# Two heads of the second batch go through the opening path, and the order of the work is set with new numbers

## The chip, the cores and the metric

One core of a Trainium2 chip runs the whole kernel. The metric is the device time of one execution in microseconds (us); lower is better. The core has a matrix engine (PE, with PEld for its weight loads), three engines for elementwise work (DVE, ACT, POOL) and SP, which here only issues DMAs.

## What is computed

Eight batches, eight heads, 576 positions, head width 64, all in float32. Attention is causal by blocks of 64 positions; its output is the input of a gated MLP that mixes positions.

```python
scores = scale * np.matmul(q, k.transpose(0, 1, 3, 2))
scores = np.where(block_i >= block_j, scores, -1000000000.0)
scores = scores - np.max(scores, axis=-1, keepdims=True)
attn = np.exp(scores)
attn = attn / (np.sum(attn, axis=-1, keepdims=True) + 1e-09)
x = np.matmul(attn, v)                   # heads side by side: 576 x 512 a batch

h = np.maximum(x @ w_in, 0.0)            # 512 -> 1024
u, v = h[..., :512], h[..., 512:]
v_n = (v - mean(v)) / np.sqrt(var(v) + 1e-06)
v_s = np.einsum('ts,bsd->btd', w_spatial, v_n) + b_spatial[None, :, None]
out = (u * v_s) @ w_out
```

## The kernel before

**Units of work.** Heads are taken in pairs, four pairs a batch. A batch is four pairs of attention and one MLP (`moe`, L1072). The MLP is made of groups of PE matmuls: five `v_group` (tile `mv`), eight `u_group` (`mu`), eight `sp_group` (`ms`, mixing of positions) and eight `out_groups` (`mo`). Most factors are split into a high and a low part, and three products stand for one of full precision.

**Two ways through attention.** Batch 0 goes through `opening` (L807): ordinary 128x128 tiles; a pair is four units (`unit(k, pr)`), each with scores (L896, L906, tile `s`), row maxima (DVE, L934, L940), exponentials (ACT), sums and scaling (POOL or ACT), transposes of the probabilities on PE (L992, tile `t`), copies of these from PSUM to `pt` (L373) and the product with the values (L1020, tile `av`). Batches 1 to 7 go through `attention` (L526). There the keys of the two heads are interleaved in blocks of 16, the masked blocks are left out, and the transpose is done in two steps: DVE turns blocks of 32x32 (L713, seven instructions a pair) and SP issues 16 DMAs of 100 KB (L723) that move the blocks from `p` to `pt`. Then follow 22 matmuls `av` (L751). Batch 1 takes q and k as they are (`plain`); later batches split them.

**Buffers.** `pt` is one tile and so is `v`; `p` has two. The 16 DMAs of a pair can start when the pair before has read `pt` for its last product. The values `v` of a pair are loaded when the pair before has read its own. Results of attention go to six tiles `x` (tag `x` of `xt_p`), which the MLP reads.

**What sets the order.** Nothing is placed by hand. Each step is an `Op` with its engine, a duration in ns, what it waits for, the buffers that it takes and gives back, and a `rank`. `Line.play` (L215) walks through time with these numbers: of the steps that could start first on an engine, the one of lowest rank goes. PE has four lanes (`S` scores, `T` transposes, `A` products with the values, `M` MLP groups in the order of a string such as `"vuvuvuvuvuuuu"`); `SLACK` says by how much a lane must be ready ahead, `op.gate` ties scores and products to how much MLP work was done (`LEAD`, `MATE_LEAD`). Where the plan sees PE wait for over some 0.9 us, `bridge` (L173) puts matmuls on an identity there (`pad`, L353, L357) whose result nobody reads. The plan only gives the order; on the chip each engine takes its queue in that order and waits on semaphores.

```python
SLACK = {"A": 2500, "S": 1200, "T": 0, "M": 100}
n = int((until - now - 300) / PAD_NS)     # L173: number of pads
```

Of the kernel before, what the change touches and what calls it, by code (L numbers as in the profile page):

```python
# [38 lines left out]
LEAD = 6.0  # L39
MATE, MATE_LEAD = 8, 6.0  # L40

# [5 lines left out]
SLACK = {"A": 2500, "S": 1200, "T": 0, "M": 100}  # L47
# [54 lines left out]
class Line:  # L102
# [112 lines left out]
    def play(self):  # L215
        while True:
# [44 lines left out]
def kernel(  # L261
# [44 lines left out]
    mask0 = ff_p.tile([P, 512], F32, tag="vl3", name="mask0")  # L306
    nc.vector.memset(mask0, 0.0)
    nc.vector.memset(mask0[0:64, 448:512], -8.0e9)
# [59 lines left out]
    mask_hold = given(r_vn, 9 * NPAIR + 14)  # L368
# [39 lines left out]
    def prep_w(hi, lo, w, rows, cols, name, rank):  # L408
# [10 lines left out]
        f_hold = mask_hold if home else Hold(r_vr, 2)  # L419
# [106 lines left out]
    def attention(b, pr):  # L526
        g = b * NPAIR + pr
        plain = b == 1
        nm = f"{b}_{pr}"
        box = {}  # L530
# [15 lines left out]
        got = add("SP", 420, load_raw, takes=[raw_hold], rank=3, size=P * 4 * Q8)  # L546
        f_hold = Hold(r_f, 1)
        got_f = add("SP", 420, load_first, takes=[f_hold], rank=3, size=P * 4 * 2 * P)
        v_hold = Hold(r_v, 1)

        def load_v():
            box["v"] = v_p.tile([P, 9, P], F32, tag="v", name=f"v_{nm}")
            nc.sync.dma_start(box["v"], v[b, pr])

        got_v = add("SP", 420, load_v, takes=[v_hold], rank=1.5, size=P * 9 * P * 4)
# [4 lines left out]
        else:  # L560
# [93 lines left out]
        for k in range(3):  # L654
            for c, (m, hd) in enumerate(SETS[k]):
                w = 32 * m + 16 if m else 32

                def rows(k=k, c=c, m=m, hd=hd, w=w):
                    if "pp" not in box:
                        box["pp"] = p_p.tile([P, 4, NT, 32], F32, tag="p", name=f"p_{nm}")  # L660
                    if ("max", k) not in box:
# [9 lines left out]
                        drops=[s_hold[k][hd % 2]], rank=1)  # L671
# [11 lines left out]
                runs_of[k].append(add("ACT", 282 + 0.845 * 4 * w, exps, after=[a], rank=2))  # L683
        for k in range(3):
# [12 lines left out]
            a = add("POOL", 200, guard, after=runs_of[k], rank=2)  # L697
            a = add("DVE", 165, turn, after=[a], rank=1.5)
            for c, (m, hd) in enumerate(SETS[k]):
# [6 lines left out]
                muls[m, hd] = add(eng, ns, scale, after=[a], rank=3)  # L706
# [3 lines left out]
        for t0, t1, of in MOVES:  # L710
# [4 lines left out]
            done.append(add("DVE", 70 + 1.05 * P * (t1 - t0), blocks, after=[muls[x] for x in of], rank=3))  # L715
        for s in range(4):
            for i in (0, 2, 1, 3):
# [9 lines left out]
                moved.append(add("SP", 635, regroup, after=done, drops=[pp_hold], rank=2, size=102400,  # L727
# [49 lines left out]
        for z, (q0, n, src) in enumerate(((0, 320, al), (320, 256, ah))):  # L777
# [16 lines left out]
            h = add("ACT", (321, 269)[z], high, after=[src], takes=takes, drops=[a_holds[z]], rank=0,  # L794
                    behind=ev[:1])
            ev.append(add("DVE", (402, 335)[z], low, after=[h], drops=[a_holds[z]], rank=0))
# [8 lines left out]
        xs_done[b, pr] = add("POOL", 271, tail, after=ev, rank=2)  # L805

    def opening():  # L807

        boxes = [{} for _ in range(NPAIR)]
# [3 lines left out]
        pp_holds = [Hold(r_pp, 7), Hold(r_pp, 9)]  # L813

        def place(k, pr):

            if k < 2:
                return k, 3 * pr, 3
# [19 lines left out]
        def load_part(pr, n):  # L838
            spans = (slice(0, 256), slice(Q0, Q0 + 256)), (slice(256, Q0), slice(Q0 + 256, KQ))
            for m, cs in enumerate(spans[n]):  # L840
                def fn(cs=cs, start=n == m == 0):
                    if start:
                        boxes[pr]["raw"] = raw_tile(pr)
                    nc.sync.dma_start(boxes[pr]["raw"][:, cs], qk[0, pr, :, cs])
# [3 lines left out]
                    "SP", 340, fn, takes=takes,  # L848
                    rank=-4 + 0.01 * len(got), size=P * 4 * (cs.stop - cs.start)))

        def load_v(pr):
            def fn():
                if pr == 1:
                    t = boxes[pr]["v"]
                elif pr == 0:
# [18 lines left out]
        load_v(3)  # L874

        def unit(k, pr):
            nm = f"0_{pr}_{k}"
            box = dict(raw=boxes[pr])
            heads = ((0, SLOTS[2 * k][1], SLOTS[2 * k][2]), (1, SLOTS[2 * k][1], SLOTS[2 * k][2]))
# [47 lines left out]
            for r, (hd, o, n, at) in enumerate(runs):  # L927
                def rows(hd=hd, o=o, n=n, at=at, r=r):
# [10 lines left out]
                    else:  # L939
                        nc.vector.tensor_tensor_reduce(  # L940
                            out=out, in0=box["s"][hd][:, o:o + n], in1=mask0[:, 512 - n:512],
# [12 lines left out]
                a = add("DVE", 76 + 1.045 * n, rows, after=[op], drops=[s_hold[hd], mask_hold], rank=-2)  # L954
                sums.append(add("ACT", 282 + 0.845 * n, exps, after=[a], rank=-1))
            n = len(runs)

            def guard():
# [5 lines left out]
            a = add("POOL", 190, guard, after=sums, rank=-1)  # L964
            a = add("DVE", 165, lambda: nc.vector.reciprocal(box["sum"][:, 4:4 + n], box["sum"][:, 0:n]),
                    after=[a], rank=-1.5)
# [465 lines left out]
```

## Time and profile before

| | us |
|---|---|
| three runs | 674.37, 675.48, 675.71 (median 675.48) |
| the profiled execution | 673.02 |
| its span, first to last instruction | 671.0 |
| PE busy in the span | 652.9 |
| DVE, ACT, POOL busy | 484.7, 374.3, 321.9 |

The profiled execution has 2.02 us outside its span, and it is 2.46 us under the median of the three runs. "Busy" counts pads too, and the end of a matmul is modelled, so two neighbouring matmuls overlap in the records: the distance from the start of one to the start of the next is what one costs in a row of equal ones. A matmul in plain float32 has two records. "Idle" in front of an instruction names what ended it.

### The profile page before, as it was taken

What the parts mean: (1) busy time and instruction counts of PE and PEld (TensorE: products, weight loads), DVE (VectorE), ACT (ScalarE), POOL (GpSimd) and SP (SyncE); (2) the same over time, 40 slices, a digit from 0 to 9 for tenths busy, and PEclk for the clock granted to TensorE, in tenths of its full rate; (3) what the DMA queues carried; (4) which work ended last, traced back from release to release, by engine and by line L of the source; (5) the groups of instructions that cost most, each with busy time, mean ns of one, the idle gap of its engine ahead of it and who ended that gap; (6) DMA issues with size and microseconds to landing.
All of it is one profiled execution on the core that took longest, in us unless ns stands there. A gap on an engine that the chain in (4) does not pass through costs nothing.

```text
span 671.0 us, 16079 instructions
## 1 busy us (share of the span) xinstructions
PE 652.9 (97%) x5670; PEld 590.1 (88%) x5670; DVE 484.7 (72%) x1353; ACT 374.3 (56%) x1067; POOL 321.9 (48%) x631
## 2 busy tenths in 40 slices
PE   7999989889999999999999999999999999999997
PEld 5588978888899888999899998999999998999997
DVE  6889879776877669677788677867787677623522
ACT  7879776554655567534665556635666455412320
POOL 4465654465565445456556454456555454411111
PEclk9999999999999999999999999999999999999999
DMA  8155577665566676566656666557656574431002
GB/s 277 64 179 175 137 200 209 191 188 143 147 175 179 189 202 169 145 164 181 175 149 169 182 190 173 159 133 198 194 142 169 151 212 124 119 93 63 1 1 71
DMA packets 48244, 103.73 MB, mean 155 GB/s; under 512 B 10146, under 2 KB 23970, under 8 KB 48164
## 3 DMA queue, kind: packets, MB, share of 16 engines
q1 hardware_dynamic: 48164, 102.71, 54.7%
q8 instruction: 45, 0.74, 0.5%
q14 instruction: 35, 0.29, 0.1%
HBM read 47.35 MB, written 9.44 MB: 85 GB/s over the span
## 4 chain that ended last, share of the span: by engine, by line
PE 73%; DMA 3%; SPq 2%; DVE 1%; POOL 1%; issue 1%; ACT 0%; POOLq 0%; ACTq 0%
PE mo L1301 14%; PE mv L1102 13%; PE ms L1249 13%; PE mu L1212 12%; PE av L751 10%; PE s L600 8%; DMA pt<-p 1%; SPq L723 1%; PE ms L1256 1%; PE ms L1254 1%; DMA v<-v 1%; POOL p L379 1%; PE s L626 1%; PE pad L357 1%; DVE p L713 0%
## 5 line engine op out<-in xcount | busy, mean ns | idle before, releaser
L379 POOL TENSOR_SCALAR p<-p,ssum 128x576 f32<-128x576 f32 (+7 forms) x256 | 151.3, 604 | 46.4 <-DMA pt<-p 20.2
L678 ACT ACTIVATE p<-p,nmax 128x320 f32<-128x320 f32 (+4 forms) x252 | 146.0, 581 | 29.9 <-DVE nmax L664 23.8
L713 DVE STREAM_TRANSPOSE p<-p 128x640 f32<-128x640 f32 (+3 forms) x196 | 119.2, 635 | 23.7 <-POOL p L379 21.4
L664 DVE CUSTOM_DVE_ANT_1 p<-s,mask 128x320 f32<-128x320 f32 (+1 forms) x224 | 112.2, 553 | 5.7 <-PE s L600 2.4
L1212 PE MATMUL mu<-x,wi_hi 128*128 128x288 f32 x512 | 109.0, 296 | 0.0
L751 PE MATMUL av<-pt,v 128*64 128x64 f32 (+2 forms) x1232 | 83.0, 290 | 8.9 <-DMA pt<-p 3.4
L751 PEld LDWEIGHTS av<-pt,v 128*64 128x64 f32 x1232 | 64.5, 137 | 29.9 <-issue 6.4
L1102 PE MATMUL mv<-wi_hi,x 128*128 128x512 f32 x256 | 85.7, 396 | 0.0
L1212 PEld LDWEIGHTS mu<-x,wi_hi 128*128 128x128 f32 x512 | 84.1, 188 | 1.5 <-ACT u L1225 0.2
L1249 PE MATMUL ms<-ws_hi,vh 128*128 128x288 f32 x256 | 77.1, 301 | 0.0
L1301 PE MATMUL mo<-gh,wo_lo 128*128 128x288 f32 x256 | 76.5, 299 | 0.0
L1301 PE MATMUL mo<-gl,wo_hi 128*128 128x288 f32 x256 | 75.9, 296 | 0.0
L1301 PE MATMUL mo<-gh,wo_hi 128*128 128x288 f32 x256 | 75.8, 296 | 0.0
L1249 PE MATMUL ms<-ws_hi,vl 128*128 128x288 f32 x256 | 75.5, 295 | 0.0
L1249 PE MATMUL ms<-ws_lo,vh 128*128 128x288 f32 x256 | 75.4, 295 | 0.0
L1212 PE MATMUL mu<-x,wi_lo 128*128 128x288 f32 x256 | 70.5, 296 | 0.0
L783 ACT CAST x<-av 128x320 fp32r<-128x320 f32 (+1 forms) x56 | 22.2, 397 | 73.7 <-PE av L751 73.7
L1102 PEld LDWEIGHTS mv<-wi_hi,x 128*128 128x128 f32 x256 | 47.8, 188 | 10.3 <-issue 0.6
L689 POOL TENSOR_SCALAR ssum<-ssum 128x4 f32<-128x4 f32 (+1 forms) x84 | 19.9, 237 | 71.8 <-ACT p L678 47.2
L800 POOL TENSOR_SCALAR xs<-x 128x128 fp32r<-128x128 f32 x28 | 9.5, 339 | 93.2 <-DVE x L786 93.2
L1271 ACT CAST gh<-u 128x288 fp32r<-128x288 f32 x64 | 26.1, 430 | 46.9 <-DVE u L1263 31.1
L1274 POOL TENSOR_TENSOR gl<-u,gh 128x288 fp32r<-128x288 f32 x48 | 37.8, 805 | 28.8 <-ACT gh L1271 27.1
(127 smaller groups left out, 1561.7 us busy)
## 6 DMA issues: line engine op xcount, KB each, us to landing
pt<-p SPq DMA_DIRECT2D x448, 100.0 KB, 2.2
v<-v SPq DMA_DIRECT2D x28, 576.0 KB, 4.7
raw<-qk SPq DMA_DIRECT2D x28, 544.0 KB, 3.7
outT<-o SPq DMA_DIRECT2D x64, 144.0 KB, 2.0
rwi<-w_in SPq DMA_DIRECT2D x8, 512.0 KB, 4.2
first<-qk SPq DMA_DIRECT2D x28, 128.0 KB, 2.3
rwo<-w_out SPq DMA_DIRECT2D x4, 512.0 KB, 4.1
rws<-w_spT SPq DMA_DIRECT2D x4, 288.0 KB, 2.9
```

The costliest lines, as they stand in the source:

```text
L379: nc.gpsimd.tensor_scalar(out=x, in0=x, scalar1=by, scalar2=1.0, op0=ALU.mult, op1=ALU.mult)
L600: nc.tensor.matmul(out(hd)[:, js], a[64 * hd:64 * hd + 64, q0:q0 + P], keys(k, hd, m, js), start=(n == 0), stop=(n == len(parts) - 1),)
L664: nc.vector.tensor_tensor_reduce(out=region(box["pp"], m, hd), in0=box["s", m, hd], in1=by.unsqueeze(1).to_broadcast([P, 4, w]), scale=-0. ...
L678: nc.scalar.activation(x, x, AF.Exp, bias=box["max", k][:, c:c + 1], scale=-1.0, accum_out=box["sum", k][:, c:c + 1],)
L713: nc.vector.transpose(x, x)
L751: nc.tensor.matmul(box["av", z][js, q0:q1], box["v"][:, c, js], move(j), start=(n == 0), stop=(n == len(todo) - 1), skip_group_check=True,)
L1102: nc.tensor.matmul(box["ps"], a, w[:, k, DH:], start=(n == 0), stop=(n == len(todo) - 1))
L1212: nc.tensor.matmul(box["ps"][:, :HT], w[:, k, ds], xts[b, k][:, j, zs], start=(n == 0), stop=(n == len(todo) - 1),)
L1249: nc.tensor.matmul(box["ps"][:, :HT], vn[k][a][:, ds], w[:, k, zs], start=(n == 0), stop=False)
L1271: nc.scalar.copy(g_box[z][0][:, dc, :], u_box["u"][:, dc, zs])
L1274: (nc.vector if dc == ND - 1 else nc.gpsimd).tensor_tensor(out=g_box[z][1][:, dc, :], in0=u_box["u"][:, dc, zs], in1=g_box[z][0][:, dc, :] ...
L1301: nc.tensor.matmul(box[ec, "ps"][:, :HT], w[:, k, es], a[:, k, :], start=(k == 0 and n == 0), stop=(last and n == 2),)
```

## The change

Pair 0 of batch 1 becomes a fifth pair of `opening` (`EARLY = 1`), behind batch 0, and leaves `attention`. Its q, k and v lie in memory as those of batch 0 do. Its raw operands take the tile of the opening's first pair again, its values the tile `v`. Of the pairs left in batch 1, pairs 1 and 3 load their values into a result tile `x` that is not in use yet (`lent`), so that these loads don't wait for the tile `v`. The mask of the opening shrinks from 512 columns to 8 that are read repeatedly. All else is the order: `LEAD` and `SLACK` are lower, the strings of MLP groups differ by batch, the weights' ranks are spread, a table `URGE` shifts the rank of some steps by stage, and three durations that the plan assumes for SP are longer.

```diff
-LEAD = 6.0
+LEAD = 5.75
+EARLY = 1
+URGE = {
+    ("first", "low"): 2,
...
+    (2, "rows"): 6,
+    (3, "scale"): 2,
+}
+ORDERS = ("vvvvvuuuuuuuu", "vvvvvuuuuuuuu", "vvuvvuvuuuuuu", "vvuvvuvuuuuuu")
+WEIGHTS = (-0.4, 0.7, 1.45, 1.45, 2.6)
-SLACK = {"A": 2500, "S": 1200, "T": 0, "M": 100}
+SLACK = {"A": 1700, "S": 1000, "T": 0, "M": 100}
-                done = self.bus + 1300
+                done = self.bus + 1450
-        v_hold = Hold(r_v, 1)
+        lent = plain and pr % 2 == 1
+        v_hold = Hold(r_x if lent else r_v, 1)
...
-                moved.append(add("SP", 635, regroup, after=done, drops=[pp_hold], rank=2, size=102400,
+                moved.append(add("SP", 640, regroup, after=done, drops=[pp_hold], rank=2, size=102400,
...
+        pairs = [(0, pr) for pr in range(NPAIR)] + [(1, pr) for pr in range(EARLY)]
...
+        for pr in range(NPAIR, len(pairs)):
+            for k in range(4):
+                unit(k, pr)
...
-        order = "vuvuvuvuvuuuu" if b else "vvvvuuuuuvuuu"
+        order = ORDERS[min(b, len(ORDERS) - 1)]
...
-        for pr in range(NPAIR):
+        for pr in range(EARLY if b == 1 else 0, NPAIR):
             attention(b, pr)
```

In the programs as built PE has 63 pads before and 4 after. With the fifth pair of the opening 25 transposes, 28 products and 10 score matmuls come, and the 12 scores, the score of the first rows and the 22 products of pair 0 of `attention` go. SP issues 16 DMAs `pt` fewer.

In the rows below, names end in the plan's own running number; `s_1_2_...` are scores of batch 1, pair 2, and `s_0_4_...`, `t_0_4_...` those of the opening's fifth pair. First PE at the end of the opening, where the first scores of batch 1 stand. Before:

```order
L600 MATMUL s_1_0_1_1_765<-raw_1_0_499 128x2x112
L600 MATMUL s_1_0_1_0_764<-raw_1_0_499 128x2x112
L600 MATMUL s_1_0_1_1_765<-raw_1_0_499 128x2x112
L1102 MATMUL mv_0_0_784<-wi_hi_120,x_0_0_301 128x512
L992 MATMUL t_0_3_3_0_790<-ident_95,p_0_1_148 128x128 x4
L1102 MATMUL mv_0_0_784<-wi_lo_121,x_0_0_301 128x512
L992 MATMUL t_0_3_3_1_803<-ident_95,p_0_1_148 128x128
```

The scores of pair 0 of batch 1 stand ahead of the MLP's first matmul. PE at the same place after:

```order
L1071 MATMUL av_0_0_3_683<-pt_0_242,v_0_0_182 64x64 x10
L1161 MATMUL mv_0_0_700<-wi_hi_120,x_0_0_0_301 128x512
L1043 MATMUL t_0_1_3_0_710<-ident_95,p_0_1_146 128x128 x4
L1043 MATMUL t_0_1_3_1_718<-ident_95,p_0_1_146 128x128
L955 MATMUL s_0_4_0_0_720<-raw_0_4_618 128x128 x2
L955 MATMUL s_0_4_0_0_720<-raw_0_4_618 128x256 x2
L1043 MATMUL t_0_2_3_0_729<-ident_95,p_0_1_146 128x128 x4
```

The MLP's first matmul stands ahead of the transposes of the opening's last units, and the fifth pair's scores come between these. Second, PE where the mixing of positions `ms` of batch 0 begins. Before:

```order
L600 MATMUL s_1_2_1_0_1305<-raw_1_2_750 128x2x112
L600 MATMUL s_1_2_1_1_1306<-raw_1_2_750 128x2x112
L353 MATMUL pad_1_1351<-ident_95 128x128 x14
L626 MATMUL s_1_2_2_1366<-first_1_2_869 128x128
L1249 MATMUL ms_0_0_0_1371<-ws_hi_124,vh_0_0_1071 128x288
```

Fourteen pads stand ahead of it. PE after, at the same place:

```order
L1271 MATMUL mu_0_1_3_1368<-x_0_1_0_322,wi_hi_120 128x288
L1271 MATMUL mu_0_1_3_1368<-x_0_2_0_361,wi_hi_120 128x288
L1271 MATMUL mu_0_1_3_1368<-x_0_3_0_375,wi_hi_120 128x288
L382 MATMUL pad_0_1437<-ident_95 128x128 x4
L1308 MATMUL ms_0_0_0_1442<-ws_hi_124,vh_0_0_1177 128x288
```

Four pads are left, the only ones of the program, and the scores of pair 2 stand earlier. Third, SP around the first sets of 16 DMAs (`pt_1_1` is pair 1 of batch 1). Before:

```order
L723 DMA pt_1_0_1032<-p_1_0_774 32x800 x7
L384 DMA rwo_0_1219<-w_out 128x1024
L384 DMA rwo_1_1237<-w_out 128x1024
L553 DMA v_1_1_1284<-v 128x1152
L723 DMA pt_1_1_1288<-p_1_1_890 32x800 x16
L384 DMA rwo_2_1418<-w_out 128x1024
```

The load of the values stands right ahead of the set, behind pair 0's set. SP after:

```order
L409 DMA rwo_0_1163<-w_out 128x1024
L760 DMA pt_1_1_1207<-p_1_1_935 32x800 x16
L409 DMA rwo_1_1358<-w_out 128x1024
L409 DMA rwo_2_1412<-w_out 128x1024
L760 DMA pt_1_2_1419<-p_1_2_1089 32x800 x16
L409 DMA rwo_3_1548<-w_out 128x1024
```

Pair 1's set is the first of the program, and no load of values stands ahead of it or of pair 2's; these were issued earlier.

## Rows read from the trace of the kernel before

**Rows 1.** The page: PE's busy time, share of the span and instructions; then PE's busy tenths and the granted clock in 40 slices of the span (9 is 90% or more).

```profile
PE 652.9 (97%) x5670; PEld 590.1 (88%) x5670; DVE 484.7 (72%) x1353; ACT 374.3 (56%) x1067; POOL 321.9 (48%) x631
...
PE   7999989889999999999999999999999999999997
...
PEclk9999999999999999999999999999999999999999
```

**Rows 2.** Busy time of each engine by stage: the stretch and its length, then us busy and instructions of PE, PEld, DVE, ACT and POOL, the granted clock (1.00 is full speed), the DMA engines' busy share and GB/s.

```profile
0.00:40.00 40.00, 36.39 (x268) 24.33 (x268) 31.20 (x122) 32.94 (x99) 20.56 (x51) 1.00 0.51 170
40.00:60.00 20.00, 19.11 (x211) 15.68 (x210) 18.67 (x52) 14.94 (x45) 10.39 (x13) 1.00 0.63 211
60.00:80.00 20.00, 20.00 (x132) 18.14 (x129) 18.45 (x51) 19.09 (x51) 14.55 (x22) 1.00 0.40 116
80.00:100.00 20.00, 17.11 (x153) 15.60 (x152) 15.32 (x43) 14.15 (x38) 9.30 (x16) 1.00 0.70 194
100.00:120.00 20.00, 18.04 (x158) 16.39 (x156) 18.55 (x51) 14.10 (x37) 9.41 (x16) 1.00 0.75 201
120.00:140.00 20.00, 16.82 (x173) 15.92 (x175) 13.02 (x38) 10.00 (x31) 11.85 (x19) 1.00 0.70 202
...
200.00:290.00 90.00, 89.18 (x835) 82.21 (x834) 66.84 (x188) 51.96 (x154) 47.57 (x95) 1.00 0.65 175
290.00:640.00 350.00, 349.88 (x3046) 321.45 (x3045) 247.31 (x668) 179.27 (x513) 162.19 (x333) 1.00 0.54 148
```

**Rows 3.** PE's waits over the whole span: the line that waited and what ended the wait, us in total, times, the longest.

```profile
PE av L751 <- DMA pt<-p: 3.4, 2, 1.9
PE av L751 <- DVE vr L1126: 2.9, 1, 2.9
PE av L751 <- DVE p L713: 1.7, 1, 1.7
...
PE av L1020 <- DVE pt L373: 0.9, 1, 0.9
PE s L906 <- DVE nmax L940: 0.9, 3, 0.5
PE av L751 <- DMA first<-qk: 0.8, 1, 0.8
PE t L992 <- POOL p L379: 0.8, 2, 0.5
PE s L906 <- DMA raw<-qk: 0.7, 1, 0.7
```

**Rows 4.** PE's timeline around two of the five stretches of pads: start, length with the last one's modelled end, instruction, count of records (two for each pad).

```profile
68.65 2.84 PE L357 MATMUL pad<-ident 128*128 128x128 f32 x24
71.25 0.38 PE L1212 MATMUL mu<-x,wi_hi 128*128 128x288 f32 x1
...
79.45 0.39 PE L1102 MATMUL mv<-wi_hi,xs 128*128 128x512 f32 x1
...
269.32 4.63 PE L357 MATMUL pad<-ident 128*128 128x128 f32 x40
273.70 0.38 PE L1249 MATMUL ms<-ws_hi,vh 128*128 128x288 f32 x1
```

**Rows 5.** What a pair costs PE. The timeline where the opening's scores begin and behind its last product, and two matmuls `mv` in a row; then PE's busy time by stage of three lines alone (stretch, length, busy us and records): L600 and L626 to 62 us, L751 from 62 to 145 us.

```profile
3.90 2.02 PE L906 MATMUL s<-raw 64*128 64x128 f32 x12
...
56.41 0.73 PE L1102 MATMUL mv<-wi_hi,x 128*128 128x512 f32 x2
...
67.27 0.40 PE L1102 MATMUL mv<-wi_hi,x 128*128 128x512 f32 x1
67.50 0.39 PE L1102 MATMUL mv<-wi_lo,x 128*128 128x512 f32 x1
...
0.00:62.00 62.00, 5.91 (x48) 1.00 0.55 182
0.00:62.00 62.00, 0.38 (x2) 1.00 0.55 182
62.00:145.00 83.00, 11.86 (x176) 1.00 0.63 178
```

**Rows 6.** The passage through `pt`, in the timelines of DVE (a pair's last block turn: that of pair 1, then of pair 2), SP (a load of values, then sets of 16 DMAs) and PE (the scores of pair 2 and the products of pairs 0 and 1; in brackets the idle time ahead and what ended it).

```profile
80.24 0.31 DVE L713 STREAM_TRANSPOSE p<-p 128x128 f32<-128x128 f32 x1
107.68 0.30 DVE L713 STREAM_TRANSPOSE p<-p 128x128 f32<-128x128 f32 x1
...
91.87 0.33 SPq L553 DMA_DIRECT2D v<-v  x1
92.42 10.52 SPq L723 DMA_DIRECT2D pt<-p  x16
...
108.17 11.08 SPq L723 DMA_DIRECT2D pt<-p  x16
...
88.87 2.96 PE L751 MATMUL av<-pt,v 128*64 128x256 f32 x44 [2.89 <-DVE vr L1126]
91.77 0.53 PE L1212 MATMUL mu<-x,wi_hi 128*128 128x288 f32 x2
92.23 0.54 PE L600 MATMUL s<-raw 64*128 64x320 f32 x2
...
104.63 0.65 PE L751 MATMUL av<-pt,v 128*64 128x256 f32 x4 [1.50 <-DMA pt<-p]
```

More of the change, by code (lines that the diff above doesn't have):

```diff
@@ L505, with urge @@
     mates = {}
+    def urge(stage):
+        return lambda what, rank: rank + URGE.get((stage, what), 0.0)
     def by_block(x):
@@ L713, in blocks @@
                 nc.vector.transpose(x, x)
-            done.append(add("DVE", 70 + 1.05 * P * (t1 - t0), blocks, after=[muls[x] for x in of], rank=3))
+            done.append(add("DVE", 70 + 1.05 * P * (t1 - t0), blocks, after=[muls[x] for x in of], rank=pace("blocks", 3)))
         for s in range(4):
@@ L803, in tail @@
             )
-        xs_done[b, pr] = add("POOL", 271, tail, after=ev, rank=2)
+        xs_done[b, pr] = add("POOL", 271, tail, after=ev, rank=pace("tail", 2))
     def opening():
-        boxes = [{} for _ in range(NPAIR)]
+        pairs = [(0, pr) for pr in range(NPAIR)] + [(1, pr) for pr in range(EARLY)]
+        boxes = [{} for _ in pairs]
         shared = {"psub": 0}
@@ L952, in exps @@
                     )
[L954 to L955 removed]
+                a = add("DVE", 76 + 1.045 * n, rows, after=[op], drops=[s_hold[hd]], rank=pace("rows", -2))
+                sums.append(add("ACT", 282 + 0.845 * n, exps, after=[a], rank=pace("exps", -1)))
             n = len(runs)
@@ L1116, in relu @@
                     nc.scalar.copy(box["vr"][:m, :], box["ps"][m:2 * m, :])
-            a = add("ACT", 480, relu, after=[end], takes=[vr_hold], drops=[hold], rank=0)
+            a = add("ACT", 480, relu, after=[end], takes=[vr_hold], drops=[hold], rank=pace("relu", 0))
             if c == FULL:
@@ L1194, in rest @@
                 nc.vector.tensor_tensor(out=vl, in0=box["vr"], in1=vh.bitcast(F32), op=ALU.subtract)
-            h = add("ACT", 520, high, after=[a], behind=vn_done[:1], takes=takes, rank=1.4)
-            l = add("DVE", 600, rest, after=[h], drops=[vr_hold], wide=True, rank=1.4)
+            h = add("ACT", 520, high, after=[a], behind=vn_done[:1], takes=takes, rank=pace("split", 1.4))
+            l = add("DVE", 600, rest, after=[h], drops=[vr_hold], wide=True, rank=pace("split", 1.4))
             vn_done.extend([h, l])
@@ L1231, in u_group @@
             takes = [u_hold] if z == 0 and dc == 0 else []
-            u_done[z, dc] = add(("ACT", "DVE"), (292, 360), relu, after=[end], takes=takes, drops=[hold], rank=0,
+            u_done[z, dc] = add(("ACT", "DVE"), (292, 360), relu, after=[end], takes=takes, drops=[hold], rank=pace("u", 0),
                                 behind=[u_done[0, 0]] if u_done else ())
@@ L1277, in rest @@
                 )
-            a = add("DVE", 355, gate, after=[end, u_done[z, dc]], drops=[hold, u_hold], rank=0)
+            a = add("DVE", 355, gate, after=[end, u_done[z, dc]], drops=[hold, u_hold], rank=pace("gate", 0))
             h = add("ACT", 336, high, after=[a], behind=g_done[z, 0][:1] if dc else ready["o"] if not b else (),
-                    takes=list(g_hold[z]) if dc == 0 else [], rank=0.5)
+                    takes=list(g_hold[z]) if dc == 0 else [], rank=pace("gh", 0.5))
             last = dc == ND - 1
```

190 lines of the change are left out of this document (118 added, 72 removed).

## The prediction

> **What bounds the kernel now.** I read the page first: PE is busy for 97% of the span, at the full granted clock in every slice [rows 1]. A busy share can hide matmuls that compute nothing, so I then read PE by stage [rows 2]: from 290 to 640 us it is idle for 0.12 us in all, and no reordering can gain there. What can be gained lies before: 2.89, 1.96 and 3.18 us idle in the stretches that begin at 80, 100 and 120 us. The list of waits says at what [rows 3]: the products with the values of `attention` (L751) waited 3.4 + 2.9 + 1.7 + 0.8 = 8.8 us, for the 16 DMAs into `pt` and what these wait for. One releaser there is named as a normalisation step on DVE (L1126), but `av` doesn't read that; the set of DMAs landed at the same time. And there are the pads: 20 of them took 273.70 - 269.32 = 4.38 us, 12 took 71.25 - 68.65 = 2.60 us [rows 4], 0.22 us each, and 63 of them 13.9 us. They count as busy, but they are waits that the plan had foreseen. So some 23 us of PE's time before 290 us go to waiting.
>
> What PE waits for is one chain. `pt` is a single buffer. Pair 0's products end at 91.77, the load of the values is issued at 91.87, pair 1's 16 DMAs go from 92.42 for 10.52 us, and its products start at 104.63, after 1.50 us idle; yet pair 1's last block turn on DVE was over at 80.24 + 0.31 = 80.55 [rows 6]. Pair 1 lost 12 us to the buffer, and each pair of the first two batches stands behind the one before.
>
> **The change part by part, against the profiled execution (673.0 us).**
>
> *The pair itself.* The opening takes PE from 3.90 to 56.41 us, 52.5 us [rows 5]. In it lie a pair of scores of `attention` (5.91 / 2 = 2.96), eleven matmuls `mv` of 67.50 - 67.27 = 0.23 us (2.5 in all) [rows 5], and PE's waits in the opening, 0.9 + 0.9 + 0.8 + 0.7 = 3.3 us [rows 3]. The rest, 43.7 us, is four pairs: 10.9 us each. In `attention` the pair cost 2.96 for scores, 0.38 for the first rows and 11.86 / 4 = 2.97 for products [rows 5], 6.3 in all. The change adds 10.9 - 6.3 = **4.6 us** of matmuls to PE. To that I add a quarter of the opening's waits, **0.8 us**, since the fifth pair goes through the same steps; it could be nothing, since MLP matmuls now stand between, or twice as much.
>
> *The pads.* 59 of 63 go, 59 x 0.22 = **-13.0 us**. This holds only if no wait takes their place; the order can't tell, so I follow the chain.
>
> *The waits at L751.* Pair 0's products started at 88.87, behind 2.89 us of waiting and the first 12 pads, 2.60 us; without these PE would have come there at 83.4. After the change pair 1's products stand at this place, behind 11.7 us more (10.9 + 0.8) and three `mu` fewer, of (79.45 - 71.25) / 60 = 0.137 us each [rows 4]: **PE comes at 94.7**. Are the data there? Ahead of pair 1's last block turn DVE has nine instructions more than before (row maxima and copies of the fifth pair, for pair 0's row maxima and block turns): between 0 and 9 x 0.36 us at DVE's mean (484.7 / 1353, [rows 1]), that is 3.2 us. I take 1.6, the middle, as some kinds go and others come: 82.2. No pair's set is ahead, so its DMAs start at once; 10.5 us for the issue, and 1.7 from its end to the products (102.94 to 104.63) [rows 6]: 94.5. PE doesn't wait, and pair 1 is 10 us ahead of before.
>
> Pair 2: behind pair 1's products (2.9) PE has 5 `mu`, 4 pads, 49 `ms`, a pair of scores and one of first rows, 0.7 + 0.9 + 6.7 + 3.0 + 0.4, so it comes 14.6 us later, at 109.3. The buffer gives: 94.7 + 2.9 + 0.3 (no load of values ahead; with it 0.65) + 10.5 + 1.7 = 110.1. PE waits 0.8. Pair 3: PE has 17.9 us of work in between (the same way, 88 MLP matmuls at 0.137 and a pair's scores and products, 5.8), and comes at 128.0. Its scores begin at some 100.6; from a pair's scores to its last block turn it took 92.23 to 107.98, 15.8 us, and a longer set 11.08 [rows 6]; 100.6 + 15.8 + 11.1 + 1.7 = 129.2. PE waits 1.2. In batch 2 PE has 16 to 22 us between products, against 10.5 + 1.7 + 2.9 + 0.3 = 15.4 for the buffer, to which stores of the MLP add some; I leave 0.6 for it. So 2.6 us remain of 8.8: **-6.2 us**. Bounds: 0 remains, or all 8.8.
>
> *Values that land early.* This is in the sum above as 0.35 us at each set; by itself it is worth nothing where PE comes later than the set.
>
> *Ranks, slack, groups of the MLP.* From 290 us on PE has no idle time to lose (0.12 us in 350, [rows 2]), and the same matmuls stay in all MLP groups: 0. The bound is on the side of a loss: with `SLACK` for products down by 0.8 us, 18 later pairs could each wait as long, 14 us; I take 0, because from 290 us on the gate by MLP work and not the slack says where products stand, and all of them found their data.
>
> *Sum.* 673.0 - 13.0 + 4.6 + 0.8 - 6.2 = 659.2 us. The profiled execution is 2.46 us under the median of the runs; with that put back the prediction is **661.7 us**.
>
> [...] PE was granted the full clock (1.00) in the stretches from 80 to 120 us too, though it stood idle there for 2.89 and for 1.50 us with no pads in that time [rows 2, 6]. [...]
>
> **The rivals.**
> 1. *The buffer stays the bound.* Loads of weights and stores of the MLP lie between the DMAs of a set and make it longer (11.08 against 10.52 already with none, [rows 6]), and PE waits for every set as before. For it: all waits at L751 were of this kind. Against: PE has 14.6 to 22 us of other work per pair. Then 8.8 us stay: 661.7 + 6.2 = 667.9.
> 2. *The vector engines are the bound, and it gets slower.* From 60 to 80 us DVE is busy for 18.45 and ACT for 19.09 of 20 us [rows 2]; the fifth pair puts copies from PSUM ahead of pair 1 there. If pair 1's block turns are late by as much as it gained, each pad comes back as a wait, the waits at L751 stay, and PE has the dearer pair on top: 673.0 + 4.6 + 0.8 + 2.46 = 680.9. It decides from where pair 1's products start later than 94.7 + 13.8 = 108.5 us. Against: DVE has only nine instructions more ahead of them, and ACT's exponentials are as many.
> [...]
> 4. *Nothing waits any more*: 661.7 - 2.6 - 0.8 = 658.3; for it: I may have put pair 2 and 3 too late.
>
> **How the numbers follow.** The forecast, 656 to 667, gets 0.70: two ways of counting (pads and waits of PE; the place of pair 1 in the chain, 10 us earlier) agree within 4 us. The buffer 0.17, of which 0.03 reach up to no change; the slower case 0.05; the clock 0.03; no waits 0.05. A measurement of this kernel tells about 0.2%, 1.4 us, from no change. Faster by more: 0.70 + 0.14 + 0.03 + 0.05 = 0.92; same 0.03; slower 0.05. The range reaches from the bounds of the sum below (no wait, the fifth pair's own waits hidden, DVE as early as before: 654) to the buffer's case with a little of the slack's loss: 671.
>
> **What would show it.** In the profile after: almost no pads; L751's first products near 94 us where they were at 88.87, but pair 1's; PE's idle time from 60 to 290 us under 5 us; SP's sets of `pt` one right behind the products before, with 10.5 to 11 us each; PE's busy time some 9 us lower; from 290 us on the same rhythm as now. Wrong would be: first products of batch 1 after 100 us, waits of 2 us or more at each set, or idle time in the late batches.

## The result and the profile after

| | before | changed |
|---|---|---|
| median of the runs, us (lowest to highest) | 674.92 (673.92 to 675.71, 4 runs) | 663.89 (663.32 to 664.99, 4 runs) |
| profiled execution, us, and its span | 673.02, 671.0 | 663.61, 661.8 |
| PE busy, us | 652.9 | 646.8 |
| span less PE's busy time, us | 18.1 | 15.0 |
| pads | 63 | 4 |

The ratio is 0.9839, with a 95% interval from 0.9819 to 0.9860: faster by 1.6%, 11.0 us between the medians. The prediction said 661.7 us and 654 to 671.

The page's first line and two of its rows in 40 slices, as in [rows 1]. One slice of the granted clock is no longer a 9.

```profile
PE 646.8 (98%) x5583; PEld 580.7 (88%) x5583; DVE 483.9 (73%) x1363; ACT 373.3 (56%) x1056; POOL 328.3 (50%) x639
...
PE   7999989999999999999999999999999999999997
...
PEclk9999989999999999999999999999999999999999
```

Busy time by stage, columns as in [rows 2]. The stretch from 80 us has a mean clock of 0.91; in the two microseconds from 88 us PE ran at 0.50. From 290 us on nothing is different: 0.10 us idle in 350.

```profile
80.00:100.00 20.00, 17.96 (x123) 16.87 (x123) 17.39 (x37) 15.09 (x37) 12.03 (x20) 0.91 0.56 151
...
290.00:640.00 350.00, 349.90 (x3011) 322.63 (x3008) 244.56 (x666) 179.49 (x509) 162.40 (x329) 1.00 0.52 145
...
88.00:90.00 2.00, 2.00 (x10) 2.00 (x10) 2.00 (x4) 1.69 (x5) 1.69 (x2) 0.50 0.65 158
92.00:94.00 2.00, 2.00 (x18) 2.00 (x17) 1.59 (x4) 1.32 (x4) 0.00 (x0) 1.00 0.63 150
```

PE's waits, as in [rows 3]. The products with the values (L788 is L751 of before) wait for 2.6 + 1.5 = 4.1 us instead of 8.8. A wait of 2.0 us is new: PE's `mu` group found no PSUM bank until DVE had evicted the group before (`u`).

```profile
PE av L788 <- DMA pt<-p: 2.6, 3, 1.2
PE mu L1271 <- DVE u L1286: 2.0, 1, 2.0
PE av L788 <- issue: 1.5, 2, 1.2
```

The passage through `pt`, the timelines of DVE, SP and PE as in [rows 6] with one row of ACT, now of pair 1, the first of batch 1 in `attention`. Its last block turn is the second of the three turns in the row at 84.78 and ends at 85.67. The set of 16 DMAs follows at 85.74, takes 10.46 us, and the products start at 99.07. Pair 1's last two scalings on ACT begin at 82.00. The `u` eviction, for which PE waits, stands behind these turns on DVE.

```profile
84.07 0.79 DVE L1221 TENSOR_SCALAR vr<-vr,st 128x512 f32<-128x512 f32 x1
84.78 1.61 DVE L750 STREAM_TRANSPOSE p<-p 128x512 f32<-128x512 f32 x3
86.32 0.41 DVE L1286 TENSOR_SCALAR u<-mu 128x288 f32<-128x288 f32 x1
...
85.74 10.46 SPq L760 DMA_DIRECT2D pt<-p  x16
...
102.17 10.04 SPq L760 DMA_DIRECT2D pt<-p  x16
...
82.00 0.95 ACT L402 ACTIVATE p<-p,ssum 128x448 f32<-128x448 f32 x2
...
86.79 0.40 PE L1271 MATMUL mu<-x,wi_hi 128*128 128x288 f32 x1 [2.04 <-DVE u L1286]
...
99.07 0.65 PE L788 MATMUL av<-pt,v 128*64 128x256 f32 x4
...
114.65 0.65 PE L788 MATMUL av<-pt,v 128*64 128x256 f32 x4 [1.17 <-DMA pt<-p]
```

**The sum against the profile.** The span fell by 9.2 us, 6.1 in busy time and 3.1 in idle time. The prediction had 13.8: 8.4 busy (13.0 of pads less 4.6 for the dearer pair) and 5.4 idle (6.2 less 0.8).

- Busy: 59 pads are gone (13.0). The slow clock adds 1.7 (10 records in two us against 18 at full clock; over 87 to 92 us). The rest, 13.0 - 6.1 - 1.7 = 5.2, is the pair and what else moved; I had 4.6.
- Idle: 4.7 came off the waits at the products, not 6.2. The `u` wait took 2.0 back. The opening's waits did not grow (0.8 in the sum).

### The profile page after: what moved, and what is told of

Same layout as the page of the kernel before. It is cut to its first block, busy times and chain, and to the rows that moved or that the text cites. A ratio compares the mean times of both kernels' runs of the same rounds, so it can differ in the third digit from the quotient of the medians.

```text
span 661.8 us, 15903 instructions
## 1 busy us (share of the span) xinstructions
PE 646.8 (98%) x5583; PEld 580.7 (88%) x5583; DVE 483.9 (73%) x1363; ACT 373.3 (56%) x1056; POOL 328.3 (50%) x639
## 4 chain that ended last, share of the span: by engine, by line
PE 85%; ACT 4%; DVE 3%; DMA 3%; SPq 3%; issue 1%; POOL 1%; POOLq 0%; ACTq 0%
PE mo L1360 15%; PE mu L1271 14%; PE mv L1161 14%; PE ms L1308 13%; PE av L788 12%; PE s L637 8%; SPq L760 3%; PE t L1043 2%; ACT p L1001 1%; DMA pt<-p 1%; PE av L1071 1%; PE ms L1315 1%; PE ms L1313 1%; DVE p L701 1%; PE s L955 1%
## 5 line engine op out<-in xcount | busy, mean ns | idle before, releaser
L404 POOL TENSOR_SCALAR p<-p,ssum 128x576 f32<-128x576 f32 (+7 forms) x263 | 157.7, 612 | 48.9 <-DMA pt<-p 25.5
L715 ACT ACTIVATE p<-p,nmax 128x192 f32<-128x192 f32 (+4 forms) x243 | 141.0, 582 | 26.5 <-DVE nmax L701 24.6
L750 DVE STREAM_TRANSPOSE p<-p 128x640 f32<-128x640 f32 (+3 forms) x189 | 115.1, 634 | 23.3 <-POOL p L404 21.4
L701 DVE CUSTOM_DVE_ANT_1 p<-s,mask 128x320 f32<-128x320 f32 (+1 forms) x216 | 108.7, 551 | 5.6 <-PE s L637 4.1
L1161 PE MATMUL mv<-wi_hi,x 128*128 128x512 f32 x256 | 84.2, 394 | 0.0
L788 PE MATMUL av<-pt,v 128*64 128x64 f32 (+2 forms) x1188 | 80.1, 290 | 4.2 <-DMA pt<-p 2.6
L788 PEld LDWEIGHTS av<-pt,v 128*64 128x64 f32 x1188 | 62.6, 137 | 23.1 <-issue 5.7
L726 POOL TENSOR_SCALAR ssum<-ssum 128x4 f32<-128x4 f32 (+1 forms) x81 | 18.4, 227 | 69.3 <-ACT p L715 53.1
```

The costliest lines, as they stand in the source:

```text
L404: nc.gpsimd.tensor_scalar(out=x, in0=x, scalar1=by, scalar2=1.0, op0=ALU.mult, op1=ALU.mult)
L701: nc.vector.tensor_tensor_reduce(out=region(box["pp"], m, hd), in0=box["s", m, hd], in1=by.unsqueeze(1).to_broadcast([P, 4, w]), scale=-0. ...
L715: nc.scalar.activation(x, x, AF.Exp, bias=box["max", k][:, c:c + 1], scale=-1.0, accum_out=box["sum", k][:, c:c + 1],)
L750: nc.vector.transpose(x, x)
L788: nc.tensor.matmul(box["av", z][js, q0:q1], box["v"][:, c, js], move(j), start=(n == 0), stop=(n == len(todo) - 1), skip_group_check=True,)
L1161: nc.tensor.matmul(box["ps"], a, w[:, k, DH:], start=(n == 0), stop=(n == len(todo) - 1))
```

## The experiments

Times are compared by the ratio to the kernel before, run on the same chip beside each kernel; its medians there were 675 to 677 us. `changed_again` and `fill_again` are the changed kernel and `fill_wait` once more. "Lost" in this table is the span less PE's busy time, plus 0.22 us for each pad; in `fill_wait` the ten extra matmuls (1.3 us) count as lost too.

| kernel | ratio, 95% interval | span | pads | lost |
|---|---|---|---|---|
| before | 1 | 671.0 | 63 | 32.0 |
| changed | 0.9839 (0.9819 to 0.9860) | 661.8 | 4 | 15.9 |
| late_fifth | 1.0032 (1.0010 to 1.0054) | 674.0 | 58 | 33.8 |
| old_numbers | 1.0040 (1.0020 to 1.0060) | 677.6 | 73 | 32.3 |
| old_ranks | 0.9966 (0.9940 to 0.9993) | 668.9 | 31 | 24.2 |
| old_groups | 0.9956 (0.9932 to 0.9980) | 672.0 | 35 | 24.5 |
| own_values | 0.9935 (0.9908 to 0.9962) | 669.9 | 30 | 21.7 |
| own_pinned | 0.9835 (0.9800 to 0.9869) | 664.8 | 4 | 18.3 |
| changed_again | 0.9815 (0.9780 to 0.9849) | 661.5 | 4 | |
| fill_wait | 0.9807 (0.9780 to 0.9834) | 660.6 | 4 | 16.5 |
| fill_again | 0.9816 (0.9789 to 0.9842) | 662.4 | 4 | |
| turns_first | 0.9801 (0.9771 to 0.9830) | 660.8 | 4 | |
| no_pads_before | 1.0016 (0.9994 to 1.0039) | 675.3 | 0 | 29.2 |
| two_queues | 1.0078 (1.0050 to 1.0106) | 679.5 | 4 | 27.4 |

### The two halves of the change, each alone

```diff
-EARLY = 1
+EARLY = 0
```

> The changed kernel with pair 0 of batch 1 back in `attention`; ranks, MLP group orders and slack stay new. The plan then holds 58 pads instead of 4. Theory (the move of the pair makes the gain): 54 pads x 0.22 = +11.9 us, the dearer passage of the pair gone (-4.2), the waits at the products with the values back from 4.2 to 8.8 us (+4.6): 663.9 + 12.3 = 676 us, and the first products of batch 1 are pair 0's. Rival (the new numbers make the gain, the move of the pair pays nothing): below 667 us, since then the sets of 16 DMAs come early whatever pair is first.

```diff
-URGE = {
...
-}
+URGE = {}
-ORDERS = ("vvvvvuuuuuuuu", "vvvvvuuuuuuuu", "vvuvvuvuuuuuu", "vvuvvuvuuuuuu")
-WEIGHTS = (-0.4, 0.7, 1.45, 1.45, 2.6)
-LEAD = 5.75
-SLACK = {"A": 1700, "S": 1000, "T": 0, "M": 100}
+ORDERS = ("vvvvuuuuuvuuu", "vuvuvuvuvuuuu")
+WEIGHTS = (0.6, 0.7, 1.45, 1.45, 2.6)
+LEAD = 6.0
+SLACK = {"A": 2500, "S": 1200, "T": 0, "M": 100}
```

> The changed kernel with pair 0 of batch 1 in the opening and the values landing early, but with the ranks, MLP group orders, weight ranks, LEAD and SLACK of before. The plan holds 73 pads. Theory (the move opens time in the chain, the new numbers are needed to fill it): 69 pads x 0.22 = +15.2 us, the wait of 2.0 us for the u eviction and the slow clock behind it (1.75 us) gone: 663.9 + 15.2 - 3.8 = 675 us. Rival (the move alone makes the gain): below 667 us.

Neither half alone gains anything: 1.0032 and 1.0040. The first theory held, in its time and in the waits at the products (8.9 us). The second held on the pads; its time was 3 us low, and the slow clock was not gone (mean granted clock 0.995). Both kernels are planned anew throughout, pads included, so they show what each half is worth to this planner and not in a fixed order. `late_fifth` keeps the chain of before: pair 0's products come at 88.33 and pair 1's at 104.60, where [rows 6] has 88.87 and 104.63. In `old_numbers` pair 1 is first, and no earlier for it. From its timelines (ACT, SP, PE):

```profile
82.91 0.66 ACT L493 CAST ws_a<-rwt 128x576 fp32r<-128x576 f32 x1
83.59 0.67 ACT L494 CAST ws_b<-rwt 1x576 fp32r<-1x576 f32 x1
...
87.23 0.67 ACT L694 ACTIVATE p<-p,nmax 128x448 f32<-128x448 f32 x1
...
88.76 0.66 ACT L381 ACTIVATE p<-p,ssum 128x448 f32<-128x448 f32 x1
...
91.17 11.17 SPq L739 DMA_DIRECT2D pt<-p  x16
...
93.56 7.53 PE L361 MATMUL pad<-ident 128*128 128x128 f32 x66
...
104.09 2.29 PE L767 MATMUL av<-pt,v 128*64 128x256 f32 x22 [2.86 <-DMA pt<-p]
```

Pair 1's last scaling on ACT stands at 88.76, behind casts of spatial weights and exponentials of pair 2; in the changed kernel the same one (128x448) is at 82.00, though the pair's last row maximum on DVE begins at nearly the same time in both (70.54 and 70.05). The set starts at 91.17 instead of 85.74, PE runs 33 pads and waits for 2.86 us more, and the products come at 104.09, as late as pair 1's were before. This is the second rival of the prediction: pads and waits stay, the dearer pair is on top. It was priced at 680.9 us; the median is 678.78 (profiled execution 679.37), although the products did not come after the 108.5 us that the rival named.

### Which of the numbers

```diff
-URGE = {
...
-}
+URGE = {}
```

> The changed kernel with the ranks of before (no urgencies by stage); MLP group orders, weight ranks, LEAD and SLACK stay new. The plan holds 31 pads. Theory (the ranks bring pair 1's block turns on DVE early; with the old ones the vector engines hold the chain): pair 1's last block turn ends near 91 us as with all numbers old, not at 85.7, its products start near 104 us; 27 pads x 0.22 = +5.9, the waits for u and the slow clock gone (-3.8), the chain 4 us later: 663.9 + 6 = 670 us. Rival (the order of the MLP groups does it): block turn at 86 us, time below 666 us.

```diff
-ORDERS = ("vvvvvuuuuuuuu", "vvvvvuuuuuuuu", "vvuvvuvuuuuuu", "vvuvvuvuuuuuu")
+ORDERS = ("vvvvuuuuuvuuu", "vuvuvuvuvuuuu")
```

> The changed kernel with the MLP group orders of before; ranks, weight ranks, LEAD and SLACK stay new. The plan holds 35 pads, none ahead of batch 1's first products. Theory (the ranks set when pair 1 is ready, the groups only what PE does meanwhile): pair 1's last block turn within 1.5 us of 85.7, its products near 99; 31 pads x 0.22 = +6.8, the wait for u gone (-3.8): 667 us. Rival (the groups set it): last block turn near 91 us, 672 us or more.

The first theory fell, and of the second only the place of the turn held (its time was 667 us, measured 672.65). Neither the ranks nor the groups alone make pair 1 early: its last block turn ends at 87.0 with the old ranks and 86.0 with the old groups, against 91.1 with all numbers old; the changed kernel itself has 85.67 and, in `changed_again`, 86.85. Both kernels lose some 8.5 us more than the changed one nonetheless (24.2 and 24.5 against 15.9), 5.9 and 6.8 us of it in more pads; 21 of the 31 and 26 of the 35 pads stand behind 210 us. So giving up either set of numbers costs much of the gain elsewhere in the plan. Which rank does what was not tried, and `LEAD`, `SLACK` and the weights' ranks were not put back alone.

### Values that land early

```diff
-        lent = plain and pr % 2 == 1
+        lent = False
```

> The changed kernel with all values of batch 1 in their own single buffer again; all else as changed, but the planner places the loads anew and holds 30 pads. Theory (a load of values between two sets costs 0.35 us of SP's time, and PE comes later than the set): the sets start 0.3 us later and no more; what the pads cost (26 x 0.22 = 5.7) the planner foresaw and the chip would not have waited: 668 us. Rival (the load itself is late, since it waits for the products before): waits at the products that name the load of values as the one that ended them, 4 us or more each: 672 us or more.

This came out in between (0.9935; 670.5 us by the ratio), and it tells little about the loads: the planner gave another order everywhere, pair 1's last block turn ended at 90.8, and 26 pads stood ahead of its products. So the same edit was made with the order held:

```diff
         def load_v():
-            if lent:
-                t = xt_p.tile([P, 2, S], F32R, tag="x", name=f"v_{nm}").bitcast(F32)
...
+            if g == NPAIR + 2:
+                values[g - 1]()
+            elif g > 2 * NPAIR:
+                own_v()
...
                     if "pt" not in box:
+                        if NPAIR + 1 < g <= 2 * NPAIR:
+                            own_v()
```

> The changed kernel with batch 1's values in their own single buffer, every other instruction in exactly the order of the changed kernel (only four loads of values stand elsewhere in SP's queue: pair 1's where pair 2's stood, the next three each right ahead of its set). Theory (early values are worth the 0.35 us of an issue, and hidden where PE comes later): the second set of batch 1 starts 0.3 us later, its products too, no more: 663.9 to 664.6 us. So what the run own_values lost came from the new plan and not from the loads. Rival (a load between two sets lengthens the set, 576 KB beside it): sets of 12 to 13 us instead of 10.1 and 11.6, 2 us at each of two products: 667 us or more.

At the second set the trace has what the rival said. The timelines of SP and PE, and a window (columns as in [rows 2]):

```profile
102.20 0.33 SPq L589 DMA_DIRECT2D v<-v  x1
102.76 12.52 SPq L766 DMA_DIRECT2D pt<-p  x16
...
116.93 4.26 PE L794 MATMUL av<-pt,v 128*64 128x256 f32 x44 [3.30 <-DMA pt<-p]
...
118.00:120.00 2.00, 2.00 (x26) 1.66 (x24) 0.38 (x1) 0.84 (x3) 0.00 (x0) 0.59 0.98 379
```

The second set takes 12.52 us with the load ahead of it and 10.04 without. PE waits for 3.30 us instead of 1.17, and the products behind run at a mean clock of 0.59 and take 4.26 us, not the 2.96 of [rows 6]. But the third set, with a load ahead of it too, takes 11.33 us, against 11.56 in the changed kernel, and in the kernel before a set right behind a load took 10.52 [rows 6]. So that the load made the second set longer is not shown. The profiled span is 3.0 us longer than the changed kernel's; the ratio beside `changed_again` (0.9835, 0.9815) does not resolve that much.

### Are pads only waits?

```diff
-        for k in range(n):
+        for k in range(0):
             out = x[:, k % 4 * P:k % 4 * P + P]
```

> The kernel before with its five stretches of pads left out (63 matmuls that feed nothing) and every other instruction in the same order. Theory (pads are waits under another name): 674.9 us within 1.5, PE idle up by 13.9 us, granted clock 1.00 as before. Rival 1 (pads keep the clock up): PE falls to half speed behind each wait as the changed kernel did at 88 us, at about 1.75 us each: up to 8.8 us slower, 684 us. Rival 2 (the pads stand where nothing had to be waited for): up to 13.9 us faster, 661 us, and the gain of the change could have been had by dropping them.

Both the theory and the first rival are half right. PE's idle time rose by 11.1 us (18.1 to 29.2) where 13.9 us of pads went: waits took the place of most of them. And PE got slow: its busy time without pads was 652.9 - 13.9 = 639.0 us and is 646.1, 7.1 us more for the same matmuls. Together that is the 4.3 us by which the profiled span is longer; the ratio is 1.0016, since most executions of the kernel before lose clock too (see *The base* below). Nothing was to be had by dropping the pads. Waits of the kernel, two lines of PE's timeline, and windows of three stretches:

```profile
PE av L751 <- DMA pt<-p: 11.1, 4, 4.4
PE s L626 <- DVE nmax L664: 3.5, 2, 3.3
PE av L751 <- DVE p L713: 3.0, 2, 1.6
PE mu L1212 <- POOL wi_lo L403: 2.1, 1, 2.1
```

```profile
141.83 5.21 PE L751 MATMUL av<-pt,v 128*64 128x256 f32 x44 [4.43 <-DMA pt<-p]
146.97 0.50 PE L1102 MATMUL mv<-wi_hi,x 128*128 128x512 f32 x1
```

```profile
104.00:108.00 4.00, 2.85 (x26) 2.37 (x28) 1.57 (x4) 0.93 (x2) 1.27 (x1) 0.69 0.92 289
...
141.00:146.00 5.00, 4.17 (x32) 3.08 (x34) 2.38 (x5) 0.94 (x2) 2.58 (x5) 0.50 0.44 138
...
224.00:230.00 6.00, 6.00 (x66) 5.02 (x68) 1.51 (x4) 0.80 (x2) 0.30 (x1) 0.72 0.50 124
```

Behind 4.43 us of waiting the products run at a clock of 0.50 and take 5.21 us. In the profiled execution of the kernel before the clock is 1.00 everywhere [rows 2]. Over whole executions the mean granted clock was 0.984 to 0.992 in the twelve without pads, and 0.989 to 1.00 in the 29 of the kernel before on the same chip: with the pads the clock is higher on the whole, but not always full.

### The slow stretch of the changed kernel

```diff
                 if n == 0:
                     box["ps"] = bank(hold, f"mu_{b}_{z}_{dc}")
+                    for _ in range(10 if b == z == dc == 0 else 0):
+                        nc.tensor.matmul(
+                            box["ps"][:, :HT], w[:, k, ds], xts[b, k][:, j, zs], start=True, stop=True,
+                        )
```

> The changed kernel with ten more matmuls of the same shape (results overwritten) ahead of the first group mu of batch 0, so that PE stands idle some 0.7 us instead of 2.04 us ahead of 86.79 us; everything else in the same order. Theory (the clock fell because PE stood idle there): granted clock 1.00 from 87 to 92 us, mu every 0.133 us instead of 0.24, PE 1.75 us earlier at the first products of batch 1 (97.3 us); their data are in at about 97.9 (end of the DMA issue at 96.20 + 1.7), so 1.2 us come through: 662.7 us. Rival (the clock fell for another reason, such as the work behind the wait): half clock there as before, 663.9 us.

> The changed kernel as it is, on the chip of the two others of this set, as their measure: 663.9 us, ratio 0.984 to the kernel before.

> The kernel with the filled wait beside the changed one on one chip. Theory (1.2 us of the slow clock come through): ratio to the kernel before 0.0018 below that of the changed kernel beside it. Rival (nothing comes through, since the sets of DMAs set the time): the same ratio.

With the wait of 2.0 us cut to 0.7 by matmuls that feed nothing, the clock is 1.00 from 88 us on in the profiles of both runs (the row of `fill_wait` below). That the wait caused the slow stretch is not shown by it, for `changed_again` is the changed kernel with its whole wait and has 1.00 there as well; its slow stretch lies in the opening. PE's timeline and two windows of `changed_again`:

```profile
87.98 0.40 PE L1271 MATMUL mu<-x,wi_hi 128*128 128x288 f32 x1 [1.99 <-DVE u L1286]
...
14.00:19.00 5.00, 4.79 (x28) 2.99 (x29) 2.23 (x7) 3.12 (x10) 3.84 (x10) 0.66 0.86 334
88.00:90.00 2.00, 2.00 (x14) 1.85 (x15) 1.75 (x4) 2.00 (x4) 1.92 (x2) 1.00 0.66 154
```

Of four profiles with this wait at about 2 us two are slow behind it (changed, `two_queues`) and two are not (`changed_again`, `own_pinned`). One thing speaks for the fill all the same: the mean clock was 0.999 or 1.00 in 11 of the 16 executions of the three kernels that have it (`fill_wait`, `fill_again`, `turns_first`) and in none of the ten of the changed kernel (0.994 to 0.997); `own_pinned`, which lacks it, has 2 of 6. What decides where the clock falls stays open.

In time the fill gives nothing that these runs resolve. In `fill_wait` PE comes to the products at 97.57 and stands there until 98.56:

```profile
97.28 0.29 PE L1275 MATMUL mu<-x,wi_hi 128*128 128x288 f32 x1
98.56 1.16 PE L788 MATMUL av<-pt,v 128*64 128x256 f32 x18 [0.99 <-DMA pt<-p]
...
88.00:90.00 2.00, 2.00 (x16) 1.85 (x16) 1.97 (x5) 1.51 (x4) 1.55 (x2) 1.00 0.63 154
```

The spans are 660.6 and 662.4 against 661.8 and 661.5 of the changed kernel, the ratios beside one another 0.9816 and 0.9815: no difference. The expected 1.2 us did not come through; the rival (the sets of DMAs set the time) holds: PE waits for the set in both runs, and `changed_again`, with no slow stretch there, waits too (0.97 us, products at 99.87).

### What sets the first products

This edit is made on top of that of `fill_wait`.

```diff
+                for t0 in (11, 24) if (b, c) == (0, 1) else ():
+                    values[t0]()
                 nc.vector.tensor_scalar(
...
+        if c == 3:
+            split = ops[1].fn
+            ops[1].fn = lambda: late.append(split)
...
+                    if (b, pr, m) == (1, 1, 3) and eng == "POOL":
+                        late.pop()()
```

> The kernel with the filled wait and, with every other instruction in the same order, two steps of the vector engines moved back behind pair 1 of batch 1: the split of a spatial weight on POOL (1.44 us at 81.10) behind pair 1's last scaling there, and a normalisation of batch 0 on DVE (0.79 us at 84.07) behind pair 1's last two block turns. Theory (the first products of batch 1 stand where pair 1's last block turn on DVE lets them): last block turn at 84.4 instead of 85.67 us, set of 16 DMAs from there, 10.5 us to issue and 1.7 to the products: products at 97.0 to 97.5 instead of 98.3 to 99.1, 662.5 us. Rival (the set's landing and not its start sets the time): products after 98 us as before and no gain.

The last block turn ends at 84.92, not at 84.4, and the products start at 98.23, not by 97.5. The rival's sentence (products after 98 us) is met, but the distance from the turn to the products is nearly the same in all of these kernels. It is 13.4 us in the changed kernel (85.67, 99.07), 13.0 in `changed_again` (86.85, 99.87), 13.4 in `own_pinned` (85.79, 99.21), 13.0 and 13.3 in the two fills (85.52, 98.56; 84.99, 98.26), 13.3 here. So the products follow the turn, at 13 us and more and not at the 12.2 of the theory, and the turn could not be moved as far as meant: on DVE, a normalisation ahead of it took 1.41 us, and 0.80 at the same place in the changed kernel. Timelines of DVE and POOL:

```profile
82.11 1.41 DVE L1237 TENSOR_SCALAR vr<-vr,st 128x512 f32<-128x512 f32 x1
...
84.85 0.50 DVE L1237 TENSOR_SCALAR vr<-vr,st 128x512 f32<-128x512 f32 x1
...
81.80 1.44 POOL L428 TENSOR_TENSOR ws_lo<-rws,ws_hi 128x576 fp32r<-128x576 f32 x1
```

This is the lowest median of all (661.40 us), with an interval that overlaps that of the changed kernel; that it beats it is not shown.

### A shorter set

```diff
-                    nc.sync.dma_start(
-                        box["pt"][32 * j:32 * j + 32, i], box["pp"][32 * i:32 * i + 32, j]
-                    )
+                    turn = (nc.sync, i, j),
+                    if plain:
+                        turn = [(nc.sync, i, j)] if s % 2 == 0 else []
+                        if i == s == 0:
+                            turn += [(nc.scalar, a, a ^ t) for t in (1, 3) for a in (0, 2, 1, 3)]
+                    for eng, i, j in turn:
+                        eng.dma_start(
+                            box["pt"][32 * j:32 * j + 32, i], box["pp"][32 * i:32 * i + 32, j]
+                        )
```

> The changed kernel with 8 of the 16 DMAs of each of batch 1's three sets issued from ACT's queue, in a row with the first one of SP. Theory (a set is as long as one queue needs to issue 16 DMAs of 0.65 us): a set takes 5.3 us from first to last issue, its products find the data there (waits of 1.2 and 0.5 us at the second and third products gone), ACT loses 8 issues per set: 662 to 664 us. Rival (a set is as long as its bytes take): the last of the set lands as late as before, 10.5 us and more behind the first issue, and ACT's loss is on top: 665 us or more.

```profile
85.76 5.95 SPq L766 DMA_DIRECT2D pt<-p  x8
...
85.76 6.26 ACTq L766 DMA_DIRECT2D pt<-p  x8
92.06 0.67 ACT L520 CAST ws_b<-rwt 1x576 fp32r<-1x576 f32 x1 [6.53 <-DMA pt<-p]
...
94.44 0.57 ACT L1179 ACTIVATE vr<-mv 128x512 f32<-128x512 f32 x1
...
95.07 0.61 PE L1277 MATMUL mu<-x,wi_hi 128*128 128x288 f32 x1 [5.55 <-ACT vr L1179]
```

The theory on the set is right: with two queues the 16 DMAs are issued in 6.3 us instead of 10.5, and over the whole run a DMA into `pt` lands in the median 2.2 us behind its issue on SP's queue and 3.5 us on ACT's, so the issue sets most of the set's length. The price on ACT was far off. ACT does nothing else for 6.53 us, the eviction of `mv` for which PE's next `mu` group needs the bank comes at 94.44, PE stands for 5.55 us and runs slow behind it (0.61 us, and 0.24 from one `mu` to the next). The first products come at 106.88, and the kernel is slower than the one before.

## Why the prediction held, and what was off in it

*The move of pair 1 in the chain* was right: first products of batch 1 are pair 1's, before 100 us, 5.6 us earlier than the same pair's were (104.63), and almost no pads. The size was off by 4.4 us at the first products (94.7 foretold, 99.07), and by 4.6 at the second (110.1, 114.65). The sum's end, 659.2, misses the profiled 663.61 by the same 4.4.

*The step that failed* is the one on pair 1's last block turn: "I take 1.6, the middle, as some kinds go and others come: 82.2." The turn ended at 85.67, 5.1 us later than before and outside the bound of 3.2. DVE's own work was sized well: it is busy for 1.7 us more ahead of the turn (68.55 and 70.28 below). What the sum left out is that the turn's inputs come later too. The longer opening was charged to PE's arrival at the products, and not to pair 1's scores, which stand on PE behind the fifth pair's and start 3.9 us later. Pair 1's last row maximum starts 5.25 us later, and from its end to the turn's end it takes 15.1 us before and 15.0 after. Rows of PE and DVE, and the windows up to the turn, before and after:

```profile
57.99 3.05 PE L600 MATMUL s<-raw 64*128 64x320 f32 x24
...
64.80 0.62 DVE L664 CUSTOM_DVE_ANT_1 p<-s,mask 128x448 f32<-128x448 f32 x1
...
0.00:80.24 80.24, 75.75 (x604) 58.34 (x605) 68.55 (x224) 67.18 (x193) 45.50 (x85) 1.00 0.52 167
...
61.87 2.86 PE L637 MATMUL s<-raw 64*128 64x320 f32 x24
...
70.05 0.62 DVE L701 CUSTOM_DVE_ANT_1 p<-s,mask 128x448 f32<-128x448 f32 x1
...
0.00:85.40 85.40, 79.89 (x637) 56.41 (x637) 70.28 (x241) 71.60 (x208) 52.10 (x99) 1.00 0.51 169
```

That the row maxima alone set the turn is not shown; the scalings on ACT and POOL stand in between, and `old_numbers` shows that they can make it later still (91.1). A second, smaller miss is the way from the turn to the products, 10.5 + 1.7 = 12.2 us in the prediction: in `fill_wait` and `fill_again`, where PE stood ready, the set released it 13.0 and 13.3 us behind the turn. In the changed kernel the data are due by that at 98.7 to 98.9, and PE came at 99.07.

*PE's side of the same place* was missed too: a wait of 2.0 us for the `u` eviction and 1.7 us lost at a clock of 0.50 were in no term. They cost little, because the data were late by nearly as much (`fill_wait`). So two misses of about 4 us fell on the same place and count once; that was luck.

*The clock.* The sum has no term for it, and the chance that the prediction gave to the clock is 0.03. The full clock of [rows 1] was that of the one profiled execution, not of the kernel: in other executions the mean granted clock goes down to 0.989. The changed kernel (2.04 us idle, then 0.50) and `no_pads_before` (4.43 us idle, then 0.50) lost clock behind a wait; `changed_again` (1.99 us idle at the same place, then 1.00) shows that such a wait need not do it. With all pads gone and no waits saved the price is 7.1 us of busy time in the profile. The changed kernel paid 1.7 in its profile.

*The pads* gave their 13.0 us, *the pair* cost about 5 for the 4.6 + 0.8 foretold, and *the waits at the products* gave 4.7 of 6.2. Two of the signs named were not met: PE is idle for 7.0 us from 60 to 290 us, not under 5, and its busy time is 6.1 us lower, not some 9.

*Early values* were priced at nothing. One profile of `own_pinned` has 3.0 us more of span, with one set 2.5 us longer and the slow clock (0.59) behind the longer wait; the other sets and the ratios do not show a price, so it stays open.

*Ranks, slack and groups* at 0 is right for the late batches (0.10 us idle in 350). As a statement on what they are worth it was wrong: without them the moved pair gains nothing (`old_numbers`).

*The base.* The profiled execution before lay 1.9 us under the median measured beside the changed kernel (674.92), the one after 0.3 us under its own. Putting back 2.46 us therefore hid 2.2 of the 4.4 us: luck again. What was put back looks like the clock. Of 82 executions of the kernel before, on the four chips of the experiments, the 8 with a mean granted clock of 1.00, as in the profiled one, have a median of 673.2 us, the 32 at 0.996 or 0.997 have 674.7, and the 40 at 0.995 or less 677.3. So the clock, which the sum left out, was in its base.

*The range.* Its lower end, 654, does not follow from the terms named with the base put back: 661.7 - 2.6 - 0.8 - 1.6 = 656.7. The time at which the data were to be there, 82.2 + 10.5 + 1.7, is 94.4 and not 94.5; nothing hangs on that.

## What to carry to other kernels

A step moved ahead in a chain comes only as early as the latest of its inputs: follow these through every engine's queue, from the first one on, and charge a delay to everything that stands behind it. Pads on PE can be waits and still earn their place (with 13.9 us of them gone, `no_pads_before` is idle for 11.1 us more and busy for 7.1 us more with the same matmuls), so ask for each pad that goes whether the wait goes too. Run the unchanged kernel a second time before a stretch of its trace is put down to a cause. And where a planner orders everything, an edit tested by planning anew tests the plan; hold the order to test the edit.

## What was not expected of the hardware

- The clock did not follow the length of an idle stretch alone: it stayed at 1.00 after 2.89 us idle [rows 2, 6], and fell to 0.50 after 2.04 us in the changed kernel, but not after 1.99 us at the same place in `changed_again`. One and the same kernel, before, had a mean clock from 0.989 to 1.00 in its executions. What tells them apart stays open.
- The same normalisation on DVE (128x512) took 0.50 and 1.41 us in one run (`turns_first`); the long one ended 0.3 us behind a split of 1.44 us on POOL that had started before it. In the changed kernel it took 0.80 us and ended 0.3 us behind the same split (81.10 to 82.54), which began earlier. That the split makes the normalisation longer is not shown: no run takes the split away.
- DMA issues on ACT's queue took the place of ACT's computing: in `two_queues` eight of them took 6.26 us, and ACT computed nothing in the 6.53 us around them.
